# Moving a load's mark, three list products and the first expert's weight splits in a fused convolution and mixture-of-experts kernel

## The chip, the core and the metric

The kernel runs on one core of one Trainium2 chip. Its time is the device time of one execution in microseconds; of the kernel before there are three runs, 1089.16 to 1090.57 us, median 1089.47 us. One more execution was taken with the profiler: 1089.97 us, of which 1088.1 us lie between its first and last instruction.

The engines: PE multiplies matrices, ACT and DVE work on vectors, POOL issues indirect transfers and does small copies, SP only issues transfers. Each engine runs its own queue in order.

## The reference

```python
# x: 8 x 2880 x 192; weight: 8 heads x 7 taps; 4 groups x 4 experts; w1 192 x 1024, w2 1024 x 192
w = softmax(weight, taps)                       # one band of 7 taps for each head of 24 columns
x = causal_conv(x, w).reshape(23040, 192)
g_idx = argmax(x @ w_group); g_w = softmax(x @ w_group)[g_idx]
e_idx = argmax(x @ w_expert[g_idx]); e_w = softmax(...)[e_idx]
out[token] = g_w * e_w * (relu(x @ w1[g_idx, e_idx]) @ w2[g_idx, e_idx])
```

Each token goes to one of 16 experts; everything is fp32.

## The kernel before

**Routing.** The 23040 tokens are cut into 192 blocks of 120, and these into 18 units of 4, 8, 12, 8, 8, 8 and then 12 blocks (units 0 to 17). `unit(u)` is a generator: it loads x (`load_unit`), convolves head by head (L516, one matmul group per head, evicted by ACT at L525), transposes (`turn_a` L540, `turn_b` L548), computes router logits (`logits_of`, L581/L584, for units 0 to 5, by quads of four blocks; `logits` L560/L562 and `logits_back` L572 from unit 6), takes argmax and softmax on DVE (L621 to L652, with the copy `ohp` on POOL, L639), stores its convolved rows to DRAM (`xcd`, L654), counts positions (L663/L664 and L667 to L706 on DVE, whose last large product is `ohl`, L695) and then makes its list of token numbers: `list_products` (L716 on PE, L724 and L726 on DVE, a scatter to the table `idtab` by POOL, L729). Up to three units are alive at once; `step()` advances them in turn by one yield.

**Experts.** A slot is 256 tokens of one expert. `open_slot` reads token numbers from the table (`idp`, L1228, SP), loads the expert's weights (`weights`) and gathers its rows (`gather`, L816, two indirect transfers on POOL). `split_one` does one of four pieces of splitting an expert's weights in a high and a low part: an ACT copy and a DVE subtraction each (L782/L783, L787/L788, L795/L796 twice). Then `turn` transposes the gathered rows (L852 on PE, L857/L858), and `hidden` (L918) and `back` do the products.

**Order at the front.** A first loop runs steps until the first five units are listed (`NEED = 5`); it takes 162 steps, k = 0 to 161. Slots 0 and 1 are opened behind it, then 108 more steps follow (`AHEAD - TB`), then the first slot's `turn`, and from there on expert work and routing steps alternate. What is traced in this order is arranged for each engine by a planner that goes by trace order and by its own estimate of when inputs are there; `hold` and `pin` keep an instruction in traced order on its engine, and `tc.issue_after(ins)` puts the instructions of a block behind `ins` on the same engine (no semaphore).

**The places of the change.** `gated_load` (L247/L248) writes a tiny mark on DVE into the x buffer, kept in order, so that the x load behind it can't start sooner; `KX` is the step at which the loads of units 7 and 8 are marked. `LATE` is the number of steps between a unit's positions and the tracing of its list (units 0 to 3; unit 4 lists at once and flushes what waits). `KPRE` gives the steps at which the first two experts' weights are loaded (60, 110) and the first expert's splits are traced (150, 155, 160; the fourth, at 162, is never reached and falls behind the 108 steps). `GPIN` names the slots whose gathers are put behind the latest traced `ohp` copy on POOL.

Of the kernel before, what the change touches and what calls it, by code (L numbers as in the profile page):

```python
# [24 lines left out]
BI = 2  # L25
# [4 lines left out]
LH = 32  # L30
# [7 lines left out]
def conv_moe_kernel(  # L38
# [10 lines left out]
    nc = tc.nc  # L49
# [41 lines left out]
    for b in range(B):  # L91
        k = b * NB
# [33 lines left out]
    QGB = 3  # L126
    AHEAD = 112
    LISTLAG = 8
    LATE = 8
    HOLD = 2  # L130
    LAG_S = 1
    PTURN = (4, 6)
# [20 lines left out]
    FRH = 0  # L153
    UG = [0, 5, 6, 1, 5, 8, 0, 5, 6, 0, 5, 7, 0, 5, 6, 2, 5, 10]
    SK = [8, 8, 6, 11, 10, 9, 9]
    KPRE = [60, 150, 155, 160, 162, 110]
    KX = 142
    SEV = 99
    TB = 4
    HGAP = 3  # L160
# [108 lines left out]
    for q, (p0, r0, n) in enumerate(((0, 0, P), (0, P, D2), (D2, P, D2))):  # L269
        c = min(q, 1)  # L270
# [14 lines left out]
    def clear_table():  # L285
# [9 lines left out]
        out=tri, in_=ones, pattern=[[1, P]], compare_op=ALU.is_gt, fill=0.0, base=0, channel_multiplier=-1,  # L295
# [12 lines left out]
    for nb in sorted({n for _, n in units}):  # L308
# [34 lines left out]
        out=sel, in_=ident.rearrange("p (e l) -> p e l", e=E), axis=AX.X, op=ALU.add)  # L343
    nc.gpsimd.iota(io[:, 0:1], pattern=[[0, 1]], base=0, channel_multiplier=1)
    nc.vector.tensor_scalar(
        out=io[:, 1:2], in0=io[:, 0:1], scalar1=LE - 1, scalar2=None, op0=ALU.bitwise_and)
# [6 lines left out]
    k = 0  # L353
    while k < E:
        n = CAPS.count(CAPS[k])
# [8 lines left out]
    for g in range(NSK):  # L364
        nc.sync.dma_start(
            out=skew[0:R, g * HG:(g + 1) * HG],
# [7 lines left out]
    for v in (3, 4):  # L374
        n = units[v][1]
# [45 lines left out]
    for h in range(H):  # L421
        nc.scalar.activation(
            out=band[0:R, h], in_=skew[0:R, h, BT - 1::-1], func=AF.Exp, bias=wm[0:R, h:h + 1],
# [27 lines left out]
        xg.append((t[:, 0:XE], t[:, XE:XE + XW]))  # L451

    GATED = (7, 8, 9, 10)
    GPIN = (2, 3)
    ohp_last = [None]
    list_last = [None]
    shared = []
    bands = {}

# [4 lines left out]
    def unit(u, pre=None):  # L464
        c0, nb = units[u]
# [40 lines left out]
        for h in range(H):  # L506
            if h:
                yield
            cs = slice(h * HC, (h + 1) * HC)
            ps = bank("c")  # L510
            if split:
                ops = ((bands["h"], xh), (bands["l"], xh), (bands["h"], xl))
            else:
                ops = ((band, xin),)
            for i, (bb, xx) in enumerate(ops):
                nc.tensor.matmul(  # L516
                    out=ps[0:BT, 0:nb * HC], lhsT=bb[0:R, h, :], rhs=xx[0:R, :, cs],
                    start=i == 0, stop=i == len(ops) - 1,
                )
            pv = ps[0:BT, 0:nb * HC].rearrange("p (b c) -> p b c", c=HC)  # L520
            xo = xc[0:BT, 0:nb, 1 + h * HC:1 + (h + 1) * HC]
            if u < CEU and h in CEH:
                nc.vector.tensor_copy(out=xo, in_=pv)
            else:
                nc.scalar.activation(out=xo, in_=pv, func=AF.Copy)  # L525
# [4 lines left out]
        k = min(range(QRING - NQ, -1, -1), key=lambda k: max(quads[k:k + NQ]))  # L530
# [45 lines left out]
        def logits_of(q):  # L576
            lgp = bank("l")
            for i in range(HQ):
                o = lgp[0:BT, 2 * i * REPL * NL:2 * (i + 1) * REPL * NL].rearrange("p (j n) -> p j n", j=2)
                for j in range(2):  # L580
                    nc.tensor.matmul(  # L581
                        out=o[:, j].rearrange("p (r n) -> p r n", n=NL), lhsT=ta[:, q, 2 * i + j],
                        rhs=wr[:, 0, 0:NL].unsqueeze(1).broadcast_to([P, REPL, NL]), start=j == 0, stop=False)
                nc.tensor.matmul(  # L584
                    out=o[:, :, 0:NL], lhsT=tb[:, q, i], rhs=wrb[:, :, 0:NL], start=False, stop=True)
            read.add((u, q))
            nc.scalar.activation(
                out=lg[0:BT, q * QB:(q + 1) * QB],
                in_=lgp[0:BT, 0:QB * REPL * NL].rearrange("p (b n) -> p b n", b=QB)[:, :, 0:NL], func=AF.Copy)
# [15 lines left out]
        Q = BT  # L605

        def bc(a, n):
# [16 lines left out]
            out=sc, in0=dd, scalar=0.0, in1=prio[0:Q].unsqueeze(1).broadcast_to([Q, M, EG]),  # L624
# [9 lines left out]
            out=ohx[0:Q], in0=ohv[:, :, 1:NG, :].rearrange("p b g e -> p g e b"),  # L634
# [59 lines left out]
        ohr = rt.tile([P, UB // BI, LH, BI], F16, name="ohr")[:, 0:NP]  # L694
# [17 lines left out]
        def list_products():  # L712
            pl = bank("l")
            nrep = REPO if u < REPU else 1
            for k in range(nb):
                nc.tensor.matmul(  # L716
                    out=pl[:, 0:nrep * LH].rearrange("p (r n) -> p r n", r=nrep),
                    lhsT=ohl[0:Q, k // BI, :, :, k % BI].rearrange("p e l -> p (e l)"),
                    rhs=ohr[0:Q, k // BI, :, k % BI].unsqueeze(1).broadcast_to([Q, nrep, LH]),
                    start=k == 0, stop=k == nb - 1,  # L720
                )
            lv5 = rt.tile([P, LH], F32, name="lv5", bufs=1)
            lsi = rt.tile([P, LH], I32, name="lsi", bufs=4)
            nc.vector.tensor_scalar(  # L724
                out=lv5, in0=pl[:, 0:LH], scalar1=0.0, scalar2=float(BIG), op0=ALU.is_equal, op1=ALU.mult)
            nc.vector.scalar_tensor_tensor(  # L726
                out=lsi, in0=pl[:, 0:LH], scalar=float(t0 - 1), in1=lv5, op0=ALU.add, op1=ALU.add)

            list_last[0] = nc.gpsimd.indirect_dma_start(  # L729
                out=TABV, out_offset=bass.IndirectOffsetOnAxis(ap=rowi.bitcast(U32), axis=0),  # L730
                in_=lsi, in_offset=None,
            )
            finished(u)

        if u < NEED - 1:
            waiting.append((done[0] + LATE, list_products))
        else:
            while waiting:
                waiting.pop(0)[1]()
            list_products()  # L740
# [62 lines left out]
    def split_one(W, k=None):  # L803

        if W["todo"] and k in (None, 4 - len(W["todo"])):
            W["todo"].pop(0)()
# [4 lines left out]
    def gather(ids, known, n=2, m=P):  # L811
        xs = xg[nslot[0] % NXG]
        nslot[0] += 1
        for t in range(n):
            with tc.issue_after(ohp_last[0].ins) if nslot[0] - 1 in GPIN else nullcontext():
                nc.gpsimd.indirect_dma_start(  # L816
                    out=xs[t][0:m, 0:XW], out_offset=None, in_=xcd[0:known, :],
                    in_offset=bass.IndirectOffsetOnAxis(ap=ids[0:m, t, 0:1].bitcast(U32), axis=0),
                    bounds_check=known - 1, oob_is_err=False,
                )  # L820
        return xs
# [328 lines left out]
    done = [0]  # L1150
# [3 lines left out]
    def step():  # L1154

        if routed[0] < NU and len(live) < lead[1] and (not live or max(live, key=lambda a: a[0])[1] >= (lead[0] or SK[min(routed[0], len(SK)) - 1])):
            u = routed[0]
            live.append([u, 0, unit(u, xin0 if u == 0 else None)])
            routed[0] += 1
        if not live:  # L1160
            return
        done[0] += 1
        while waiting and waiting[0][0] <= done[0]:
            waiting.pop(0)[1]()
        cur = live.pop(0)
        cur[1] += 1
        try:
            next(cur[2])
            live.append(cur)
        except StopIteration:  # L1170
            pass
# [110 lines left out]
    def open_slot(i):  # L1282
        if i >= len(plan) or i in opened:
            return
        pi, v, at, n, m = plan[i]
        if closing:
            wait[0] -= 1
            if wait[0] <= 0 or closing[0] == pi:
                open_portion(closing.pop())
        while pi not in idps:  # L1290
            step()
            if closing:
                open_portion(closing.pop())
        rate[0] = max(
            [(stages_to(portions[q][0]) - done[0]) / (max(starts[q] - MARGIN - i, 1) * 2 * NF)
             for q in starts if q not in idps] + [0.0])
        if at:
            W = opened[i - 1][0]
        elif pi == LASTP:
            W = weights(*tail_regs(lambda c: tab[0][0:1, v, c:c + 1], 2))  # L1300
        else:
            e = portions[pi][1][v][0]
            if pi == 0 and e in pre:
                W = pre.pop(e)
                with tc.issue_after(opener[0].ins):
                    while W["more"]:
                        W["more"].pop(0)()
            elif i <= 3:
                with tc.issue_after(opener[0].ins):
                    W = weights(e * D, e * F)  # L1310
            else:
                W = weights(e * D, e * F)
        lists(pi, v + IDN)
        ids = idps[pi][v][:, at:at + n]
        known = sum(n for _, n in units[:portions[pi][0]]) * BT
        opened[i] = (W, ids)
        gathered[i] = gather(ids, known, n, m)

    pre = {}
    rooms, factors = {}, {}  # L1320
    k = 0
    while routed[1] < portions[0][0]:
# [16 lines left out]
        clear_half(0)  # L1339
    open_slot(0)  # L1340
    open_slot(1)
    for k in range(AHEAD - TB):
        step()
    while opened[0][0]["todo"]:
        split_one(opened[0][0])
    if TB:
# [201 lines left out]
```

## Time and profile before

| | us |
|---|---|
| median of three runs | 1089.47 |
| profiled execution | 1089.97 |
| its span | 1088.1 |
| PE busy | 1043.7 (96%) |
| DVE busy | 677.6 (62%) |
| ACT busy | 618.4 (57%) |
| POOL busy | 531.7 (49%) |

The time that PE does not work lies nearly all at the front, while the first units are routed and the first experts start, and at the very end. Idle time of an engine counts only where the next work of PE waits for it. In the rows below "idle before" in brackets is the time that the engine waited, and the arrow names what ended the wait.

### The profile page before, as it was taken

To read this page: it belongs to the slowest core of one execution; us is meant where nothing else is said; L and a number is where in the kernel's file an instruction comes from. 1 tells how busy PE (TensorE), PEld (TensorE's weight loads), DVE (VectorE), ACT (ScalarE), POOL (GpSimd) and SP (SyncE) were. 2 spreads that over 40 slices of the span, in tenths; PEclk is the share of its full clock that TensorE was granted. 3 is DMA by queue.
4 is the path that set the end of the run, shared out by engine and by line. 5 is a ranking of instruction groups with operands and counts; after the bars stand their busy time and mean duration, and the time that the engine had idled before them with its cause. 6 is when DMAs were issued, how large, how long until landed. Compare 5 with 4: busy or idle time off the path is not lost.

```text
span 1088.1 us, 20687 instructions
## 1 busy us (share of the span) xinstructions
PE 1043.7 (96%) x7116; PEld 980.7 (90%) x7116; DVE 677.6 (62%) x1650; ACT 618.4 (57%) x1380; POOL 531.7 (49%) x677
## 2 busy tenths in 40 slices
PE   6878999999999999999999999999999999999996
PEld 5756888998999899899999999999999999999996
DVE  4667878886777766656464646556466465655652
ACT  5566687886666645545453645545455455555552
POOL 3233343543333446655554553555556656667542
PEclk9989999999999999999999999999999999999998
DMA  8866897886674343432231313133132233233200
GB/s 210 233 174 161 194 271 201 230 224 186 161 167 133 93 116 89 115 85 65 75 83 53 100 41 90 56 95 97 42 96 69 77 92 104 66 87 98 68 26 23
DMA packets 120281, 126.40 MB, mean 116 GB/s; under 512 B 20619, under 2 KB 106896, under 8 KB 120170
## 3 DMA queue, kind: packets, MB, share of 16 engines
q1 hardware_dynamic: 72682, 71.24, 24.7%
q0 software_dynamic: 24160, 35.99, 11.9%
q10 hardware_dynamic: 23328, 17.80, 6.7%
q8 instruction: 57, 0.93, 0.4%
q14 instruction: 54, 0.44, 0.1%
HBM read 89.03 MB, written 36.07 MB: 115 GB/s over the span
## 4 chain that ended last, share of the span: by engine, by line
PE 76%; DMA 7%; DVE 6%; issue 5%; ACT 3%; POOL 3%; POOLq 0%; SPq 0%; ACTq 0%; DVEq 0%
PE ph L888 26%; PE po L902 10%; PE pm L902 7%; PE ph L918 7%; PE po L906 5%; PE po L936 4%; PE pm L906 3%; PE pm L516 3%; PE po L940 2%; DMA out<-ys,idp 2%; DMA xin<-in_x 2%; PE ph L852 1%; POOL out L955 1%; POOL xg L816 1%; PE pm L540 1%
## 5 line engine op out<-in xcount | busy, mean ns | idle before, releaser
L955 POOL DMA_INDIRECT out<-ys,idp x187 | 214.2, 1146 | 258.2 <-DVE ys L965 203.9
L892 DVE SCALAR_TENSOR_TENSOR hl<-ph,hh 128x360 fp32r<-128x360 f32 (+13 forms) x328 | 189.5, 584 | 197.9 <-ACT hh L891 174.8
L891 ACT ACTIVATE hh<-ph 128x360 fp32r<-128x360 f32 (+13 forms) x328 | 166.3, 515 | 207.9 <-PE ph L888 182.4
L816 POOL DMA_INDIRECT xg<-xcd,idp x187 | 226.7, 1212 | 70.6 <-issue 36.6
L902 PE MATMUL po<-cw,hh 128*120 128x384 f32 (+6 forms) x656 | 209.9, 357 | 0.0
L888 PE MATMUL ph<-xa,wf 128*128 128x360 f32 (+13 forms) x656 | 182.3, 359 | 0.0
L888 PE MATMUL ph<-xc,wf 128*128 128x360 f32 (+13 forms) x656 | 176.4, 350 | 1.7 <-DVE xc L864 1.7
L906 PE MATMUL po<-cw,hl 128*120 128x192 f32 (+6 forms) x656 | 164.7, 251 | 0.0
L902 PE MATMUL pm<-cw,hh 128*120 128x384 f32 (+6 forms) x440 | 147.1, 356 | 0.0
L936 PE MATMUL po<-cw,hh 128*128 128x384 f32 x400 | 134.5, 386 | 0.1
L888 PEld LDWEIGHTS ph<-xc,wf 128*128 128x128 f32 x656 | 118.8, 189 | 11.1 <-DVE xc L864 1.9
L906 PEld LDWEIGHTS po<-cw,hl 128*120 128x120 f32 (+6 forms) x656 | 121.7, 186 | 3.0
L918 PE MATMUL ph<-xa,wf 128*128 128x256 f32 x600 | 118.8, 306 | 5.1 <-DVE wf L783 2.2
L902 PEld LDWEIGHTS po<-cw,hh 128*120 128x120 f32 (+6 forms) x656 | 120.4, 184 | 2.8
L888 PE MATMUL ph<-lts,wf 128*128 128x360 f32 (+13 forms) x328 | 115.0, 351 | 0.0
L906 PE MATMUL pm<-cw,hl 128*120 128x192 f32 (+6 forms) x440 | 110.4, 251 | 0.0
L888 PEld LDWEIGHTS ph<-xa,wf 128*128 128x128 f32 x656 | 100.9, 189 | 1.3
L940 PE MATMUL po<-cw,hl 128*128 128x192 f32 x400 | 101.6, 254 | 0.0
L918 PEld LDWEIGHTS ph<-xa,wf 128*128 128x128 f32 x600 | 88.7, 192 | 11.6 <-DVE wf L783 2.4
L924 DVE SCALAR_TENSOR_TENSOR hl<-ph,hh 128x512 fp32r<-128x512 f32 x100 | 68.2, 686 | 44.0 <-ACT hh L923 38.2
L918 PE MATMUL ph<-xb,wf 128*128 128x256 f32 x400 | 81.9, 286 | 2.8 <-DVE xb L864 2.0
L923 ACT ACTIVATE hh<-ph 128x512 fp32r<-128x512 f32 x100 | 59.5, 598 | 43.6 <-PE ph L918 40.1
(277 smaller groups left out, 1905.2 us busy)
## 6 DMA issues: line engine op xcount, KB each, us to landing
rawc<-in_moe_w SPq DMA_DIRECT2D x66, 384.0 KB
raw<-in_moe_w SPq DMA_DIRECT2D x33, 512.0 KB
xcd<-xc ACTq DMA_DIRECT2D x13, 1085.6 KB
raw<-in_moe_w SPq DMA_DIRECT2D x33, 256.0 KB
xin<-in_x SPq DMA_DIRECT2D x7, 1134.0 KB
xin<-in_x SPq DMA_DIRECT2D x5, 1039.5 KB
xg<-xcd,idp POOLq DMA_INDIRECT x187
out<-ys,idp POOLq DMA_INDIRECT x187
```

Source lines behind the costliest of these rows:

```text
L816: nc.gpsimd.indirect_dma_start(out=xs[t][0:m, 0:XW], out_offset=None, in_=xcd[0:known, :], in_offset=bass.IndirectOffsetOnAxis(ap=ids[0:m, ...
L888: nc.tensor.matmul(out=hp, lhsT=W[wgt][:, fs], rhs=xx[:, 0:n], start=i == 0, stop=i == len(ops) - 1)
L891: nc.scalar.activation(out=hh, in_=hp, func=AF.Relu)
L892: nc.vector.scalar_tensor_tensor(out=hl, in0=hp, scalar=0.0, in1=hh.bitcast(F32), op0=ALU.max, op1=ALU.subtract,)
L902: nc.tensor.matmul(out=oo[t][0:m, 0:2 * D], lhsT=hh[:, ts], rhs=cw[:, f].rearrange("p a d -> p (a d)"), start=f == 0, stop=False,)
L906: nc.tensor.matmul(out=oo[t][0:m, 0:D], lhsT=hl[:, ts], rhs=cw[:, f, 0, :], start=False, stop=f == NF - 1,)
L918: nc.tensor.matmul(out=hp[:, j], lhsT=wgt[:, fs], rhs=xx, start=i == 0, stop=i == len(ops) - 1)
L923: nc.scalar.activation(out=hh, in_=hp, func=AF.Relu)
L924: nc.vector.scalar_tensor_tensor(out=hl, in0=hp, scalar=0.0, in1=hh.bitcast(F32), op0=ALU.max, op1=ALU.subtract,)
L936: nc.tensor.matmul(out=oo[t][:, 0:2 * D], lhsT=hh[:, j, ts], rhs=cw[:, f].rearrange("p a d -> p (a d)"), start=f == 0, stop=False,)
L940: nc.tensor.matmul(out=oo[t][:, 0:D], lhsT=hl[:, j, ts], rhs=cw[:, f, 0, :], start=False, stop=f == NF - 1,)
L955: nc.gpsimd.indirect_dma_start(out=outviews[nscat[0] % len(outviews) if view is None else view], out_offset=bass.IndirectOffsetOnAxis(ap=i ...
```

## The change

- `KX` from 142 to 130. The mark for x of units 7 and 8 is traced behind unit 3's positions and unit 4's first logits, where it was behind unit 4's argmax.
- `LATE` from 8 for all to (8, 8, 14, 10). Unit 2's list is traced at step 127 instead of 121, unit 3's at 137 instead of 135.
- `BEHIND`: on PE the list products of unit 1 go behind the latest traced logits, those of units 2 and 3 behind the latest logits and the latest convolution. Counted through the generators these are: unit 1 behind unit 3's first logits; unit 2 behind unit 3's second logits and unit 5's second head; unit 3 behind unit 4's second logits and unit 5's sixth head.
- The four splits of the first expert are not traced at steps 150 to 160, but at steps 2, 8, 14 and 20 of the 108 that follow the opening.
- The gathers of slots 0 and 1 are traced only once a new `ohp` copy is (unit 5's, at step 13 of the 108) and go behind it on POOL.

```diff
-    LATE = 8
+    LATE = (8, 8, 14, 10)
+    BEHIND = ((), ("l",), ("l", "c"), ("l", "c"))
-    KPRE = [60, 150, 155, 160, 162, 110]
-    KX = 142
+    KPRE = [60, 999, 999, 999, 999, 110]
+    FIRST = (2, 8, 14, 20)
+    KX = 130
-    GPIN = (2, 3)
+    GPIN = (0, 1, 2, 3)
+    recent = {}
...
-                nc.tensor.matmul(
+                recent["c"] = nc.tensor.matmul(
                     out=ps[0:BT, 0:nb * HC], lhsT=bb[0:R, h, :], rhs=xx[0:R, :, cs],
...
-                nc.tensor.matmul(
+                recent["l"] = nc.tensor.matmul(
                     out=o[:, :, 0:NL], lhsT=tb[:, q, i], rhs=wrb[:, :, 0:NL], start=False, stop=True)
...
         def list_products():
             pl = bank("l")
             nrep = REPO if u < REPU else 1
-            for k in range(nb):
+            with ExitStack() as queued:
+                for kind in BEHIND[u] if u < len(BEHIND) else ():
+                    queued.enter_context(tc.issue_after(recent[kind].ins))
+                for k in range(nb):
...
-            waiting.append((done[0] + LATE, list_products))
+            waiting.append((done[0] + LATE[u], list_products))
...
-        gathered[i] = gather(ids, known, n, m)
+
+        def fetch():
+            gathered[i] = gather(ids, known, n, m)
+
+        if i < 2:
+            fetches.append(fetch)
+        else:
+            fetch()
...
     open_slot(0)
     open_slot(1)
+    newest = ohp_last[0]
     for k in range(AHEAD - TB):
         step()
+        while fetches and ohp_last[0] is not newest:
+            fetches.pop(0)()
+        if k in FIRST:
+            split_one(opened[0][0])
     while opened[0][0]["todo"]:
         split_one(opened[0][0])
```

## Rows read from the trace of the kernel before

**Rows 1.** Windows: busy us of each engine (instructions), granted clock, DMA share, GB/s.

```profile
63.40:74.30 10.90, 6.44 (x28) 5.41 (x28) 4.74 (x17) 4.40 (x11) 1.25 (x3) 0.69 0.83 268
74.30:93.20 18.90, 16.55 (x120) 10.86 (x119) 13.65 (x56) 14.28 (x36) 9.47 (x10) 1.00 0.61 148
59.40:98.20 38.80, 29.35 (x188) 20.98 (x186) 27.09 (x102) 25.18 (x62) 12.12 (x15) 0.91 0.64 173
98.20:200.00 101.80, 95.86 (x734) 87.59 (x735) 81.95 (x192) 75.80 (x147) 39.14 (x38) 0.99 0.88 229
600.00:800.00 200.00, 200.00 (x1290) 195.35 (x1289) 113.90 (x240) 106.86 (x246) 107.42 (x147) 1.00 0.29 76
```

**Rows 2.** Waits of PE, 36 to 100 us: total us, times, longest us.

```profile
PE ph L516 <- DMA xin<-in_x: 4.5, 1, 4.5
PE pm L716 <- DVE ohl L695: 2.8, 2, 1.5
PE ph L918 <- DVE xa L858: 1.7, 1, 1.7
PE ph L716 <- DVE ohl L695: 1.7, 1, 1.7
```

**Rows 3.** Timeline of PE, 55 to 74 us: start, us, line, what.

```profile
55.59 0.84 PE L716 MATMUL pm<-ohr,ohl 120*128 120x192 f16 x8 [1.25 <-DVE ohl L695]
56.28 0.58 PE L581 MATMUL pm<-wr,ta 128*120 128x100 f32 x4
...
61.41 0.66 PE L581 MATMUL po<-wr,ta 128*120 128x100 f32 x4
...
62.69 0.72 PE L516 MATMUL ph<-wf,band 126*120 126x288 f32 x2
67.88 1.28 PE L516 MATMUL ph<-xin,band 126*120 126x288 f32 x2 [4.46 <-DMA xin<-in_x]
68.96 1.49 PE L716 MATMUL pm<-ohr,ohl 120*128 120x192 f16 x8
...
71.24 0.97 PE L581 MATMUL pm<-wr,ta 128*120 128x100 f32 x4
...
73.51 0.93 PE L516 MATMUL pm<-xin,band 126*120 126x288 f32 x2
```

**Rows 4.** Timeline of DVE, 54 to 67 us: units 3 and 4, mark, splits.

```profile
54.84 0.69 DVE L695 TENSOR_TENSOR ohl<-ohp,oh 120x1024 f16<-120x1024 f16 x1
...
57.95 0.32 DVE L621 TENSOR_REDUCE mx<-lg 120x40 f32<-120x160 f32 x1 [1.06 <-ACT lg L587]
...
60.80 0.07 DVE L248 MEMSET xin<- 1x2 f32 x2
...
61.35 1.22 DVE L783 TENSOR_TENSOR wf<-raw,wf 128x1024 fp32r<-128x1024 f32 x1
...
62.97 1.21 DVE L788 TENSOR_TENSOR wf<-raw,wf 64x1024 fp32r<-64x1024 f32 x1
...
66.11 0.69 DVE L695 TENSOR_TENSOR ohl<-ohp,oh 120x1024 f16<-120x1024 f16 x1
```

**Rows 5.** Timeline of SP at the mark: the load of unit 7's x.

```profile
60.92 0.34 SPq L236 DMA_DIRECT2D xin<-in_x  x1
```

**Rows 6.** Timeline of all engines: a split's copy, POOL beside DVE, the last split.

```profile
59.99 1.07 ACT L782 ACTIVATE wf<-raw 128x1024 fp32r<-128x1024 f32 x1
...
74.21 2.80 POOL L401 TENSOR_SCALAR wf<-ident 64x1024 fp32r<-64x1024 f32 x1 [1.56 <-DMA idtab<-lsi,rowi]
74.37 1.07 DVE L622 TENSOR_TENSOR dd<-lg,mx 120x160 f32<-120x160 f32 x1
...
95.09 0.95 DVE L796 TENSOR_TENSOR cw<-rawc,cw 128x768 fp32r<-128x768 f32 x1
```

**Rows 7.** Timeline: the last gather of slots 0 and 1, the first transpose of slot 0.

```profile
82.23 1.01 POOL L816 DMA_INDIRECT xg<-xcd,idp  x1 [0.30 <-issue]
...
93.16 0.27 PE L852 MATMUL pm<-ident,xg 128*128 128x128 f32 x1
```

More of the change, by code (lines that the diff above doesn't have):

```diff
@@ L714, in list_products @@
             nrep = REPO if u < REPU else 1
-            for k in range(nb):
[L716 to L721, printed above, removed]
+            with ExitStack() as queued:
+                for kind in BEHIND[u] if u < len(BEHIND) else ():
+                    queued.enter_context(tc.issue_after(recent[kind].ins))
+                for k in range(nb):
+                    nc.tensor.matmul(
+                        out=pl[:, 0:nrep * LH].rearrange("p (r n) -> p r n", r=nrep),
+                        lhsT=ohl[0:Q, k // BI, :, :, k % BI].rearrange("p e l -> p (e l)"),
+                        rhs=ohr[0:Q, k // BI, :, k % BI].unsqueeze(1).broadcast_to([Q, nrep, LH]),
+                        start=k == 0, stop=k == nb - 1,
+                    )
             lv5 = rt.tile([P, LH], F32, name="lv5", bufs=1)
@@ L1316, in open_slot @@
         opened[i] = (W, ids)
-        gathered[i] = gather(ids, known, n, m)
+        def fetch():
[4 more added lines that the diff above has]
+            fetch()
     pre = {}
+    fetches = []
     rooms, factors = {}, {}
```

## The prediction

> **What bounds the kernel now.** I read the page's busy shares first, then the windows, PE's waits, and the timelines of PE, DVE, SP and POOL where those waits lie. PE is the bound: from 600 to 800 us it is busy 200.00 of 200.00 us at full clock [rows 1], so work that it does earlier at the front comes off the end, if nothing takes it back in between. At the front it is not full: from 63.4 to 74.3 us it is busy 6.44 of 10.90 us at a mean granted clock of 0.69, from 74.3 to 93.2 us 16.55 of 18.90 [rows 1]. The waits name the causes [rows 2]: 4.5 us for the x load of unit 7, three waits for `ohl` before list products (2.8 us in two, 1.7 us in one), 1.7 us for the subtraction `xa` of the first slot.
>
> The timeline shows how the longest arises. The convolution of unit 7 stands on PE ahead of unit 4's list and starts at 67.88, after 4.46 us of waiting [rows 3]; its load was issued at 60.92 [rows 5], right behind the mark at 60.80 [rows 4]. From mark to convolution that is 7.08 us, and the mark is what set it. Behind the wait PE runs at the lower level, 1.2 GHz instead of 2.4: the 8-block list takes 1.49 us at 68.96 and 0.84 at 55.59, and the logits with their second half go from 71.24 to 73.51 (2.27 us), where the same go from 61.41 to 62.69 (1.28 us) [rows 3].
>
> **The change part by part.**
>
> *The mark.* It stands behind what is traced before it: now behind unit 4's argmax, at 60.80. Moved to step 130 it comes behind unit 3's positions, whose last large product ends at 54.84 + 0.69 = 55.53 [rows 4]; I put it at 55.6, and x is usable at 55.6 + 7.1 = 62.7. PE has run out of other work at 67.88 - 4.46 = 63.42 [rows 3], 1.2 us sooner with the next part, so 62.2. About 0.5 us of the wait is left: gain 4.46 - 0.5 = 3.9 us. It is worth this only if PE isn't stopped there by something else, namely unit 4's list, whose `ohl` ends at 66.11 + 0.69 = 66.80 [rows 4]: see the splits. The moved load issues the same transfers on SP; the queue holds nothing between them and the opening, and DMA is used 0.83 in the stretch that they leave [rows 1].
>
> *The clock.* If PE doesn't stand still for 4.46 us, I expect no fall. From 67.88 to 73.51 it does one convolution, the list, another convolution and two halves of logits in 5.63 us [rows 3]. At full clock: two convolutions at half of 1.08, the list 0.69 (from 55.59 to 56.28), the logits 1.28 [rows 3], together 3.05. Gain 2.6 us; nothing if a like wait stays.
>
> *The list products.* Unit 3's now stands ahead of unit 4's second logits: PE waits 1.25 us for `ohl`, does the list at 55.59, and only then the logits at 56.28 [rows 3], so that DVE stands idle for them until 57.95 [rows 4]. Behind the logits the list has their 1.28 us as cover: gain 1.2 us on PE, and unit 4's argmax can start when unit 3's `ohl` is done, at about 56.0, so 1.9 us sooner. For units 1 and 2 the edges ask for what the order of before has already: what they name was issued ahead of these lists. Their waits, 1.5 and 1.7 us [rows 2], I leave as they are: gain 0, at best 3.2 if the later place of unit 2's list reorders more, at worst -1.7 if it does so the other way (the longest such wait once more).
>
> *The splits, where they go from.* Two subtractions, 1.22 and 1.21 us, stand at 61.35 and 62.97 inside unit 4's chain to `ohl` [rows 4]. Without them and with the argmax 1.9 us sooner, `ohl` ends at 66.80 - 2.43 - 1.9 = 62.5, as early as PE gets to the list. So the x wait is not replaced by a wait for `ohl`; the two belong together, and if the splits stayed, some 2.4 us of the 3.9 would be lost again. The opening, behind unit 4's list, comes some 6 us sooner.
>
> *The splits, where they go to.* The fourth one's subtraction, 0.95 us at 95.09 [rows 6], stands now ahead of the first slot's `xa`, for which PE waits 1.7 us [rows 2]: gain 0.95, and up to 2.6 if the rest of that wait and its slow clock go too. The others come new into the stretch between opening and first slot: on DVE 1.22 + 1.21 + 0.95 = 3.4 us. DVE is busy 13.65 of 18.90 us there, ACT 14.28 of 18.90 [rows 1]. Bounds: 0, if they fall into the idle 5.25 us; 3.4, if all lie on the path. I take 2.4, since the two that stand in unit 4's chain today were both on the path in whole and the two traced at steps 2 and 8 come ahead of unit 5's argmax in the same way. The ACT copies (1.07 us for the largest [rows 6]) I count at nothing: the copies precede the subtractions and the evictions that they hold up have several PSUM buffers; if ACT bound the stretch they would cost about as much as the subtractions, which the upper end covers.
>
> One row of this stretch speaks against the place: `clear_half` on POOL runs 2.80 us from 74.21, and the DVE subtraction that starts beside it at 74.37 takes 1.07 us [rows 6], where an instruction over the same 120x160 values takes 0.32 [rows 4]; it is 0.75 longer, but it ends at 75.44, long before POOL does at 77.01. The splits' subtractions will stand near this instruction. The Trainium skill says in "SBUF — State Buffer", section "SBUF: two separate sides", that a DVE operation with two SBUF inputs and a GpSimd operation that reads SBUF share one pair of ports as an exclusive lock for the whole instruction. By that rule DVE should have been shut out for all of POOL's 2.80 us, so the trace agrees that there is a price, not with its size.
>
> *The gathers.* Today the last gather of slots 0 and 1 is issued at 82.23 and slot 0's rows are first used at 93.16 [rows 7], a cover of 10 us. Behind unit 5's copy they shift with the opening and with unit 5, both sooner. Cost 0; without that cover each gather costs about the 1.01 us of its issue on POOL [rows 7] and its landing.
>
> *Sum.* 3.9 + 2.6 + 1.2 + 0.95 - 2.4 = 6.25 us. The profiled execution of 1089.97 us becomes 1083.7; it lies 0.5 us above the median of the runs, so I forecast 1083.2. DVE allows this: from 59.4 to 98.2 us it is busy 27.09 of 38.80 us [rows 1], so up to 11.7 us could go before it is full. Behind 98.2 us the relations stay: splits, loads and gathers of later slots hang on the first slot's progress, and DMA, 0.88 busy up to 200 us [rows 1], gets two x loads and the first weight buffers sooner. That is the least certain step.
>
> **The rivals.**
>
> *Both waits for unit 1 and 2 lists go too.* The new edges leave PE other work there: 1083.2 - 3.2 = 1080.0. Against it: the named work was done already.
>
> *The lock in whole.* A subtraction of the splits waits out `clear_half`, 2.80 us instead of the 0.75 of the row [rows 6], and unit 5 behind it: 2.05 us more, 1085.3. It is the rule named above as a mechanism of this kernel; the row bears it out only in part.
>
> *The wait travels with the mark.* PE's order is planned with an estimate of the load that is too short: today unit 7's convolution is reached 63.42 - 60.80 = 2.6 us after the mark. If the plan keeps that distance, the 4.46 us and the slow clock stay: 0 + 0 + 1.2 + 0.95 - 2.4 = -0.25, so 1090.2, or 1089.7 against the median. Against it: the hole that drew the convolution there is the wait for unit 4's `ohl`, and ahead of it PE has other work without a gap.
>
> *Slower.* The plan sets that convolution right behind the mark, at about 56 us on PE, ahead of unit 3's list and unit 4's logits: then PE waits the whole 7.08 us there, 2.6 more than today, unit 4's chain waits with it, and the splits cost their 2.4: 1089.97 + 2.6 - 1.2 - 0.95 + 2.4 = 1092.8, or 1092.3 against the median. It decides from where less than 2.6 us of PE work lie between mark and convolution.
>
> **How the numbers follow.** Forecast 0.56, lists 0.08, lock 0.10, travelling wait 0.14, slower 0.12. The measurement can tell about 0.2% of this kernel, 2.2 us, from no change. Faster by more: 0.56 + 0.08 + 0.10 = 0.74; within: 0.14; slower: 0.12. The range: from 1083.2 the free splits give 2.4 less and the rest of the `xa` wait 1.6 less, 1079.2, and with some of the list waits 1078; upwards the splits in whole and the lock give 1086.3, and the travelling wait is taken in with a little room, 1090.5. What is left out is the slower case and the far end of the list case.
>
> **What would show it.** Right: the x load issued near 56 us, PE's wait for x under 1 us, a granted clock of 1.00 through 60 to 80 us, unit 4's logits ahead of unit 3's list, the opening's read of the table some 6 us sooner, slot 0's first transpose near 87 us instead of 93.16, and the same distance of about 6 us still there at 200 and at 600 us. Wrong: a wait for x of 4 us or more anywhere, a clock under 0.9 in that stretch, DVE full from opening to first slot with PE waiting for it, or a gain at the first slot that is gone by 200 us, which would mean that DMA or DVE behind it set the pace.

## The result, and the profile after

The changed kernel takes 1081.7 us in the median of four runs (1080.2 to 1082.43), where the kernel before took 1090.02 us beside it (1089.16 to 1092.17): a ratio of 0.991, 95% interval 0.9886 to 0.9933. The forecast was 1083.2 us, so direction and range hold, and the gain is 8.3 us where 6.25 were summed. The profiled execution is 1081.58 us long, 1079.7 of it between first and last instruction. Three single runs of the kernels below took 1661 to 2081 us; no ratio counts them.

Windows of the changed kernel, over stretches of [rows 1] and over 140 to 200 us; columns as there, with the granted clock and the DMA share ahead of GB/s.

```profile
63.40:74.30 10.90, 7.89 (x54) 6.12 (x54) 8.35 (x24) 9.25 (x21) 5.10 (x4) 1.00 0.44 103
74.30:93.20 18.90, 15.24 (x105) 9.74 (x105) 12.86 (x50) 13.35 (x33) 6.13 (x8) 0.91 0.65 163
600.00:800.00 200.00, 200.00 (x1287) 195.37 (x1286) 113.30 (x238) 105.18 (x242) 105.14 (x144) 1.00 0.29 81
140.00:200.00 60.00, 60.00 (x482) 54.77 (x482) 48.30 (x111) 47.65 (x96) 25.10 (x23) 1.00 0.92 240
```

From 63.4 to 74.3 us the granted clock is 1.00 instead of 0.69, and PE gets through 54 instructions where it did 28. From 74.3 to 93.2 us the stretch became worse: 15.24 us busy instead of 16.55, clock 0.91 instead of 1.00. PE is still the bound later (200.00 of 200.00 us).

Waits of PE in the changed kernel, 36 to 100 us: total us, times, longest us.

```profile
PE pm L722 <- ACT lg L576: 1.9, 1, 1.9
PE pm L722 <- DVE ohl L698: 1.8, 2, 1.2
PE ph L563 <- ACT ta L544: 1.8, 1, 1.8
PE ph L666 <- DVE cum L644: 1.7, 1, 1.7
PE ph L722 <- DVE ohl L698: 1.3, 1, 1.3
```

Against [rows 2]: the wait for x is gone from the list, the waits for `ohl` are shorter (1.8 and 1.3 us instead of 2.8 and 1.7), the waits for `ta` and `cum` (1.8 and 1.7 us) are new, and that for `lg` has grown from 0.6 to 1.9 us. All of PE's waits in this stretch, the smaller ones with them, come to 9.9 us, where they were 14.0. (The changed file's lines stand 2 to 6 further down: L516 is L519, L716 is L722, L918 is L924.)

Where the lead arises shows when the same event of both traces is set side by side (start in us):

| event | before | after | lead |
|---|---|---|---|
| unit 3's first argmax | 44.13 | 44.35 | -0.2 |
| unit 4's first argmax | 57.95 | 54.20 | 3.8 |
| unit 7's first convolution | 67.88 | 60.47 | 7.4 |
| unit 4's list on PE | 68.96 | 63.47 | 5.5 |
| table read by the opening | 74.15 | 69.62 | 4.5 |
| slot 0's first transpose | 93.16 | 89.81 | 3.4 |
| slot 0's first expert product | 95.54 | 91.17 | 4.4 |
| 1st scaling of an output tile (ACT) | 117.15 | 111.14 | 6.0 |
| 3rd | 134.14 | 130.46 | 3.7 |
| 11th | 193.20 | 186.09 | 7.1 |
| 34th | 351.12 | 344.09 | 7.0 |
| 180th | 1047.86 | 1039.09 | 8.8 |

So there are three phases: 5.5 us won up to unit 4's list, 2.1 of them lost by the first slot, and over 5 us won after that, with a loss of 2.3 us between the first and the third scaling.

PE and DVE of the changed kernel up to unit 4's list (start, us, line, what).

```profile
48.61 0.07 DVE L250 MEMSET xin<- 1x2 f32 x2
...
48.87 0.57 PE L584 MATMUL pm<-wr,ta 128*120 128x100 f32 x4
...
50.78 1.18 PE L722 MATMUL ph<-ohr,ohl 120*128 120x192 f16 x12 [1.35 <-DVE ohl L698]
...
53.09 0.64 PE L584 MATMUL pm<-wr,ta 128*120 128x100 f32 x4
...
54.20 0.32 DVE L624 TENSOR_REDUCE mx<-lg 120x40 f32<-120x160 f32 x1
...
55.10 0.69 DVE L698 TENSOR_TENSOR ohl<-ohp,oh 120x1024 f16<-120x1024 f16 x1
...
55.85 0.84 PE L722 MATMUL pm<-ohr,ohl 120*128 120x192 f16 x8 [0.59 <-DVE ohl L698]
...
59.84 0.19 PE L666 MATMUL ph<-cum,tri 120*128 120x16 bf16 x1
...
60.11 0.17 DVE L670 TENSOR_TENSOR off<-ph,eoff 128x16 f32<-128x16 f32 x1 [1.50 <-PE ph L667]
...
60.47 0.70 PE L519 MATMUL ph<-xin,band 126*120 126x288 f32 x2
...
62.72 0.69 DVE L698 TENSOR_TENSOR ohl<-ohp,oh 120x1024 f16<-120x1024 f16 x1
...
63.47 0.84 PE L722 MATMUL pm<-ohr,ohl 120*128 120x192 f16 x8
```

The mark stands at 48.61 us, ahead of unit 2's `ohl` (49.77). Unit 4's second quad of logits, which stood behind unit 3's list (56.28 [rows 3]), now begins ahead of unit 2's list (48.87) and goes on ahead of unit 3's (53.09). Unit 4's argmax starts at 54.20, ahead of unit 3's `ohl` (55.10). Unit 7's convolution finds x there at 60.47, and unit 4's list runs at full clock (0.84 us, before 1.49 [rows 3]).

All engines of the changed kernel, from opening to the first slot.

```profile
66.24 1.22 DVE L789 TENSOR_TENSOR wf<-raw,wf 128x1024 fp32r<-128x1024 f32 x1 [1.48 <-ACT wf L788]
...
67.13 1.19 POOL L735 DMA_INDIRECT idtab<-lsi,rowi  x1 [5.24 <-DMA idtab<-lsi,rowi]
...
69.69 2.80 POOL L403 TENSOR_SCALAR wf<-ident 64x1024 fp32r<-64x1024 f32 x1 [1.37 <-DMA idtab<-lsi,rowi]
69.80 1.11 DVE L632 TENSOR_TENSOR oh<-sc,mx 120x160 f32<-120x160 f32 x1
...
71.34 0.87 ACT L801 ACTIVATE cw<-rawc 128x768 fp32r<-128x768 f32 x1
71.45 1.06 DVE L653 TENSOR_SCALAR sg<-ss 120x8 f32<-120x8 f32 x1
71.86 0.93 DVE L802 TENSOR_TENSOR cw<-rawc,cw 128x768 fp32r<-128x768 f32 x1
...
73.38 0.32 ACTq L657 DMA_DIRECT2D xcd<-xc  x1
...
81.61 0.42 ACT L528 ACTIVATE xc<-ph 120x288 f32<-120x288 f32 x1 [2.42 <-DMA xcd<-xc]
82.32 0.40 DVE L624 TENSOR_REDUCE mx<-lg 120x60 f32<-120x240 f32 x1 [5.27 <-ACT lg L576]
```

Windows of the changed kernel, 4 us each, over the same place.

```profile
68.00:72.00 4.00, 2.49 (x14) 1.50 (x13) 3.93 (x11) 3.98 (x9) 2.63 (x2) 1.00 0.34 23
72.00:76.00 4.00, 1.63 (x16) 0.94 (x19) 3.90 (x19) 3.20 (x10) 2.99 (x4) 0.90 0.93 265
76.00:80.00 4.00, 4.00 (x31) 2.29 (x24) 0.91 (x3) 3.08 (x5) 2.83 (x4) 0.68 1.09 268
80.00:84.00 4.00, 2.09 (x20) 1.75 (x18) 1.58 (x5) 1.95 (x6) 0.00 (x0) 1.00 0.46 128
```

This is where the lead shrinks. While the splits run, ACT is busy 3.98 and DVE 3.93 of 4.00 us, and PE only 2.49, then 1.63, and the clock behind it is 0.68. Unit 5's convolved rows are stored at 73.38, in ACT's queue behind the splits' copies, and behind weight loads that SP issued from 70.12 us on. A later eviction waits for that store until 81.61, and from 80 to 84 us no engine is busy for much over half of the time.

### The profile page after: what moved, and what is told of

The parts are those of the page before. It is cut to its first block, busy times and chain, and to the rows that moved or that the text cites. A ratio compares the mean times of both kernels' runs of the same rounds, so it can differ in the third digit from the quotient of the medians.

```text
span 1079.7 us, 20690 instructions
## 1 busy us (share of the span) xinstructions
PE 1041.8 (96%) x7116; PEld 979.3 (91%) x7116; DVE 675.8 (63%) x1650; ACT 618.2 (57%) x1380; POOL 534.0 (49%) x677
## 4 chain that ended last, share of the span: by engine, by line
PE 85%; DVE 6%; DMA 4%; ACT 2%; issue 1%; POOL 0%; SPq 0%; POOLq 0%; DVEq 0%; ACTq 0%
PE ph L894 28%; PE po L908 10%; PE ph L924 9%; PE pm L908 8%; PE po L942 6%; PE po L912 5%; PE pm L912 4%; PE pm L519 4%; PE po L946 3%; DMA out<-ys,idp 2%; PE ph L858 1%; PE pm L543 1%; PE pm L722 1%; DMA xcd<-xc 1%; DMA xin<-in_x 1%
## 5 line engine op out<-in xcount | busy, mean ns | idle before, releaser
L961 POOL DMA_INDIRECT out<-ys,idp x187 | 216.5, 1158 | 264.2 <-DVE ys L971 210.3
L924 PE MATMUL ph<-xa,wf 128*128 128x256 f32 x600 | 118.4, 305 | 2.4 <-DVE wf L789 2.4
L924 PEld LDWEIGHTS ph<-xa,wf 128*128 128x128 f32 x600 | 88.2, 191 | 8.6 <-DVE wf L789 2.8
L924 PE MATMUL ph<-xb,wf 128*128 128x256 f32 x400 | 81.5, 285 | 3.3 <-DVE xb L870 2.0
```

The costliest lines, as they stand in the source:

```text
L924: nc.tensor.matmul(out=hp[:, j], lhsT=wgt[:, fs], rhs=xx, start=i == 0, stop=i == len(ops) - 1)
L961: nc.gpsimd.indirect_dma_start(out=outviews[nscat[0] % len(outviews) if view is None else view], out_offset=bass.IndirectOffsetOnAxis(ap=i ...
```

## The experiments

All ratios are to the kernel before on the same chip, with 95% intervals; the gain is (1 - ratio) x 1090 us. The line of the whole change is that of its second measurement, beside the experiments. The three sets of experiments ran on three chips, so kernels of different sets are compared by their ratios alone. A kernel with parts alone is the changed file with the other parts set back.

| kernel | ratio | interval | gain, us | PE's wait for x |
|---|---|---|---|---|
| whole change | 0.991 | 0.9895 to 0.9926 | 9.8 | none |
| without the mark | 0.9977 | 0.9961 to 0.9992 | 2.5 | 4.0 |
| without the lists | 0.9957 | 0.9944 to 0.997 | 4.7 | none |
| without the splits | 0.9925 | 0.9907 to 0.9943 | 8.2 | none |
| without the gathers | 0.9936 | 0.9917 to 0.9955 | 7.0 | none |
| mark alone | 0.995 | 0.9936 to 0.9965 | 5.5 | none |
| lists alone | 0.9963 | 0.9945 to 0.9981 | 4.0 | 3.7 |
| splits alone | 0.9962 | 0.9941 to 0.9984 | 4.1 | 0.2 |
| mark and lists | 0.9931 | 0.9905 to 0.9958 | 7.5 | none |
| whole, mark at step 138 | 0.9973 | 0.995 to 0.9996 | 2.9 | 3.8 |
| whole, splits at 36 to 54 | 0.9904 | 0.9889 to 0.9919 | 10.5 | none |
| that, mark at step 138 | 0.9947 | 0.9922 to 0.9971 | 5.8 | 2.9 |

The start of an execution varies by some us from one to the next (unit 3's first argmax lies between 42.09 and 48.32 us in the profiled ones), so where times of different traces are compared below, they are counted from that event.

First theory, the prediction's: the mark is the largest part, the lists a small one, and the splits cost something at their new place. Rival: the lists or the splits carry the gain. Four kernels put one part of the changed kernel back.

**Without the mark.**

```diff
-    KX = 130
+    KX = 142
```

> The changed kernel with only the mark put back (step 142). First theory, the wait for x is the largest part of the gain: the mark stands behind unit 4's argmax again, near 58 us, x lands near 65, PE waits 2 to 4 us for it with unit 4's list behind, and runs some 4 us at the lower clock; 1085 to 1087 us, against 1081.7 with the whole change. Rival, PE would stand still there anyway for unit 4's ohl (ready at 63.4 in the changed kernel): the wait only changes its name, 1082 to 1083 us.

Measured: 0.9977. The mark is worth some 7 us here (9.8 - 2.5), somewhat above the first theory's 3.3 to 5.3 and far from the rival's 0.3 to 1.3. Timeline of DVE and PE of this kernel:

```profile
61.10 0.07 DVE L250 MEMSET xin<- 1x2 f32 x2
...
69.58 0.75 PE L519 MATMUL ph<-xin,band 126*120 126x288 f32 x2 [3.98 <-DMA xin<-in_x]
70.14 1.48 PE L722 MATMUL pm<-ohr,ohl 120*128 120x192 f16 x8
```

The old picture is back: a wait of 3.98 us, and the list behind it at the lower level (1.48 us).

**Without the lists.**

```diff
-    LATE = (8, 8, 14, 10)
-    BEHIND = ((), ("l",), ("l", "c"), ("l", "c"))
+    LATE = (8, 8, 8, 8)
+    BEHIND = ((), (), (), ())
```

> The changed kernel with LATE 8 for all and no BEHIND. First theory, unit 4's logits ahead of unit 3's list are worth 1.2 us of PE and bring unit 4's argmax 1.9 us sooner or more: without them 1083 to 1085 us. Rival, the time that unit 4 gains is lost again behind the opening, where unit 5's stored rows hold the evictions of unit 8: 1081.5 to 1082 us.

Measured: 0.9957. The lists are worth about 5 us, where the prediction had 1.2. From unit 3's to unit 4's first argmax this kernel takes 14.02 us, the whole change 9.85, the kernel before 13.82. This distance goes with the lists: it is 9.75 to 10.71 in all kernels of the study that have them and 13.80 to 14.06 in all that don't. No run separates the later steps (`LATE`) from the edges (`BEHIND`).

**Without the splits.**

```diff
-    KPRE = [60, 999, 999, 999, 999, 110]
-    FIRST = (2, 8, 14, 20)
+    KPRE = [60, 150, 155, 160, 162, 110]
+    FIRST = ()
```

> The changed kernel with the first expert's splits back ahead of the opening. First theory, both places cost about the same on the path (2.4 us in unit 4's chain, 2.4 us in unit 5's) and only the fourth split's 0.95 us and its slow clock at the first slot differ: 1082.5 to 1084.5 us. Rival one, the new place is the dearer (ACT is full from 68 to 72 us in the changed kernel and PE waits 1.8 us for it): 1079.5 to 1081 us. Rival two, the mark is worth nothing without the splits moved: 1087 us or more.

Measured: 0.9925, 1.6 us above the whole change, with intervals that overlap. PE waits 1.51 us for unit 4's `ohl` and 1.6 us for `xa` in this kernel, and not in the whole change, but the fuller stretch behind the opening is absent too. So what the splits' new place is worth in the whole change is not settled by this run. It does settle something about the store of unit 5's rows. ACT of this kernel:

```profile
71.08 0.32 ACTq L657 DMA_DIRECT2D xcd<-xc  x1
...
80.45 0.42 ACT L528 ACTIVATE xc<-ph 120x288 f32<-120x288 f32 x1 [1.39 <-DMA xcd<-xc]
```

No copy of a split stands between opening and store here, but three weight loads (69.38 to 70.65 us on SP) do. The store comes 27.03 us behind unit 3's argmax (whole change 29.03), and an eviction still waits 1.39 us for it.

**Without the gathers.**

```diff
-    GPIN = (0, 1, 2, 3)
+    GPIN = (2, 3)
...
-        if i < 2:
+        if i < 0:
             fetches.append(fetch)
```

> The changed kernel with the gathers of slots 0 and 1 issued at the opening and not put behind the copy. They then stand ahead of unit 5's copy on POOL and hold it by about 5 us; DVE idles 5 us at that place in the changed kernel. First theory, this cover hides it: 1081.2 to 1082.2 us, no change. Rival, unit 5's list and everything in DVE's order behind it come later: 1083 to 1085 us.

Measured: 0.9936, 2.8 us above the whole change, at the edge of what the intervals separate. POOL and DVE of this kernel:

```profile
79.06 1.01 POOL L822 DMA_INDIRECT xg<-xcd,idp  x1 [0.31 <-issue]
80.12 0.30 POOL L642 CAST ohp<-ohx 120x128 f16<-120x128 bf16 x1
...
80.45 0.69 DVE L698 TENSOR_TENSOR ohl<-ohp,oh 120x1024 f16<-120x1024 f16 x1 [3.27 <-POOL ohp L642]
```

With the four gathers in front, unit 5's copy is done only at 80.12, and DVE waits 3.27 us for it. In the whole change the copy is at 72.55 and `ohl` at 76.36. The edge has a use that the prediction didn't give it: it lets the copy past the gathers.

The second set took the whole change once more as a reference, each of two parts alone, and the splits later.

> The changed kernel once more, unaltered, for a comparison on the same chip with the three below. All theories: 0.988 to 0.993 of the kernel before, 8 to 13 us less.

Measured: 0.991 (1078.42 to 1082.48 us). Its trace has the same waits (9.4 us of PE's in 36 to 100 us).

**The mark alone** (kernel before, with `KX` at 130).

```diff
-    KX = 142
+    KX = 130
```

> The kernel before with the mark alone moved to step 130. First theory, the mark is worth most of the gain by itself: PE does unit 7's convolutions where it waited, the clock stays, unit 4's list goes ahead as soon as its ohl is there (66.8 in the kernel before, so 2 us sooner): 4 to 6 us less than before. Rival, mark and splits need each other (the wait for ohl takes the place of the wait for x): 1 to 2.5 us less.

Measured: 0.995. The prediction had said that mark and splits belong together and that some 2.4 us would be lost with the splits in unit 4's chain. PE does wait for `ohl` there, 1.05 us, and unit 4's list runs at the lower level (1.46 us), but 5.5 us remain.

**The lists alone** (kernel before, with `LATE` and `BEHIND`).

```diff
-    LATE = 8
+    LATE = (8, 8, 14, 10)
+    BEHIND = ((), ("l",), ("l", "c"), ("l", "c"))
```

> The kernel before with the lists' new places alone. First theory: unit 4's argmax comes 3 us sooner, but the wait for x behind the late mark stays and takes it back: 0 to 1.5 us less than before. Rival, the mark itself stands behind unit 4's argmax and moves with it, so that the gain goes through: 2.5 to 4 us less.

Measured: 0.9963. The mark, still traced behind unit 4's argmax, follows it to 56.62 us; the wait for x is 3.7 us.

**The splits later**, at steps where unit 5's rows are already stored.

```diff
-    FIRST = (2, 8, 14, 20)
+    FIRST = (36, 42, 48, 54)
```

> The changed kernel with the first expert's four splits at steps 36, 42, 48 and 54 behind the opening instead of 2, 8, 14 and 20. In the changed kernel DVE idles 5.3 us from 77 to 82 us, ACT is full from 68 to 72, and unit 5's store takes 8.2 us from 73.4 because four weight loads, set free by the splits, go ahead of it. First theory, the splits and the loads that they set free crowd unit 5: 2 to 4 us less than the changed kernel. Rival, the store is slow for the gathers and the loads need the early splits: no change, or up to 2 us more where the second expert's weights come too late.

Measured: 0.9904, 1078.61 us (1077.85 to 1081.74). Windows of this kernel over the place of the loss:

```profile
68.00:72.00 4.00, 1.31 (x12) 0.70 (x14) 3.69 (x20) 2.58 (x8) 3.20 (x3) 0.92 0.59 94
72.00:76.00 4.00, 4.00 (x26) 1.75 (x18) 2.61 (x4) 3.95 (x6) 3.08 (x4) 0.65 0.63 166
76.00:80.00 4.00, 3.85 (x30) 3.09 (x29) 3.79 (x10) 4.00 (x12) 1.36 (x3) 1.00 0.98 316
80.00:84.00 4.00, 3.92 (x25) 1.58 (x24) 3.83 (x20) 1.98 (x7) 1.53 (x3) 1.00 0.56 164
```

Unit 5's rows are stored at 69.16 us, no eviction waits for that, and PE is busy 3.92 of 4.00 us at 80 to 84 instead of 2.09. The store comes 27.07 us behind unit 3's argmax, as in the kernel without the splits' move, but here the weight loads follow it:

```profile
74.06 0.48 SPq L767 DMA_DIRECT2D raw<-in_moe_w  x1
```

So of the eviction's wait, the weight loads ahead of the store are the likely part, beside the copies that make it later. PE's wait for `ta` and the fall of the clock do not go away: PE is busy 1.31 of 4.00 us at 68 to 72 (a wait of 2.6 us for `ta`), and the clock behind it is 0.65. Counted from unit 3's first argmax, the 34th scaling comes at 296.23 us, against 299.74 and 298.80 in the two traces of the whole change; at the 60th 0.6 and 1.3 us of that are left.

What the place costs can be read from unit 4's list on PE to slot 0's first transpose: 22.39 to 24.58 us in the five traces with the splits ahead of the opening, 25.64 to 28.78 in the seven with splits at steps 2 to 20, and 24.15 and 25.34 in the two with later ones. So the loss behind the opening came in good part from the place of the splits. In the timed runs the intervals of this kernel and of the whole change overlap widely; a better kernel is not shown.

The last set asked how far the mark's place decides, and whether parts add. It ran on a chip where the kernel before itself varied from 1083.2 to 1095.62 us, and its intervals are wider.

**The mark at step 138**, close to where the prediction had put it.

```diff
-    KX = 130
+    KX = 138
```

> The whole change with the mark at step 138 instead of 130; on DVE it then stands behind unit 3's list numbers, near 57.4 us, where the changed kernel has it at 48.61 (and where the prediction had put it at 55.6). First theory: all that counts is whether x is there when PE is free for it; a load takes some 7 to 8 us, so x is usable at 64.5 to 65.5, PE is free at about 61 to 63, and it waits 2 to 4 us with a slow clock behind: 2 to 4 us above the whole change, 1083.5 to 1085.5. Rival: the early mark has a price of its own, since the x loads at 55 to 63 us slow down the table scatters and the opening; then the later mark gives an opening sooner by 1 to 2 us and no loss: 1080 to 1081.5.

Measured: 0.9973. Timeline of DVE and PE of this kernel:

```profile
61.43 0.07 DVE L250 MEMSET xin<- 1x2 f32 x2
...
70.08 1.28 PE L519 MATMUL ph<-xin,band 126*120 126x288 f32 x2 [3.78 <-DMA xin<-in_x]
```

This execution started later: its unit 3's argmax is at 48.32, so the mark stands 13.1 us behind it (whole change 4.3, before 16.7; the prediction's 55.6 would be 11.5). PE waits 3.78 us for x, and most of the gain is gone. The rival had a true part: with the mark early, the table's scatters run against the x loads. DMA issues of the whole change, then of this kernel, 44 to 76 us: count and median us from issue to landing. In each, the median is that of one scatter, unit 2's; the trace doesn't tell when the others landed.

```profile
idtab<-lsi,rowi POOLq DMA_INDIRECT x4, 6.6
```

```profile
idtab<-lsi,rowi POOLq DMA_INDIRECT x4, 2.2
```

But the price is outweighed: from unit 3's argmax the table is read after 25.27 us in the whole change and after 27.84 here.

**Late splits, mark at step 138.**

> As the kernel with splits at steps 36 to 54 (1078.6), with the mark at step 138 instead of 130. First theory: again 2 to 4 us above the same kernel with the early mark, 1080.5 to 1082.5. Rival: the scatters are freed and the opening comes sooner, 1077 to 1078.5.

Measured: 0.9947, with a wait of 2.9 us for x: the same answer at the other place of the splits. The sizes, 4.7 us here and 6.9 us above, are larger than the 2 to 4 expected, though the intervals are too wide to exclude 4.

**Mark and lists**, with splits and gathers as before.

> The mark and the lists of the change; splits and gathers where they stood before. The two alone gave 5.5 and 4.0 us. Theory that the parts add: 9.5 us, 1080.5, so that the new places of splits and gathers are worth nothing by themselves. Rival, from the two runs that put one of them back (1083.7 and 1084.1): they are worth 2 to 4 us together, since the splits' subtractions again stand in unit 4's chain to ohl (2.4 us) and POOL does gathers ahead of unit 5's copy: 1083.5 to 1086. Unit 4's ohl should end near 65 us and PE wait about 2 us for it if the rival holds.

Measured: 0.9931, a gain of 7.5 us; the interval, 4.6 to 10.4 us, takes in both the sum of the two alone (9.5 us) and 4 us less than that. Of what the rival named, PE's wait for unit 4's `ohl` is there, 1.51 us, and it ends at 63.30 us on PE.

**The splits alone.** The expectation names the gathers too; in the kernel they stood where they were before, only the splits had moved.

```diff
-    KPRE = [60, 150, 155, 160, 162, 110]
+    KPRE = [60, 999, 999, 999, 999, 110]
+    FIRST = (2, 8, 14, 20)
```

> The kernel before with the new places of splits and gathers alone; mark and lists as before. The prediction's steps: 0.95 gained at the fourth split, 2.4 lost at the new place, the x wait and the slow clock as before: 1.4 us slower, 1091. Parts that add (whole change less mark and lists alone, 9.8 - 5.5 - 4.0 = 0.3): 1089 to 1090. Rival, that unit 4's chain is freed of 2.4 us and this comes through by itself: 1086.5 to 1088.

Measured: 0.9962, 4.1 us faster, where the prediction's own steps give 1.4 slower. PE of this kernel:

```profile
66.11 1.46 PE L722 MATMUL pm<-ohr,ohl 120*128 120x192 f16 x8 [1.52 <-DVE ohl L698]
...
70.46 0.72 PE L519 MATMUL ph<-xin,band 126*120 126x288 f32 x2 [0.19 <-DMA xin<-in_x]
```

With unit 4's chain free of splits, PE's order puts the list ahead of unit 7's convolution, and the wait for x falls to 0.19 us although the mark is as late as before (62.07, which is 16.6 us behind unit 3's argmax; before 16.7). PE still waits 1.52 us for `ohl`, and the list runs at the lower level (1.46 us).

**What the table says.** The parts don't add. Lists and splits alone gave 4.0 and 4.1 us, but together, with the gathers and without the mark, 2.5: a gap of 5.6 us, where the intervals together leave some 3.5. Mark, lists and splits alone sum to 13.6 us, the whole gave 9.8; this difference alone would be at the edge of the intervals. The likely reason, which no run isolates, is that the planner makes a new order for each combination, and that whether PE meets a convolution whose x isn't there depends on that order.

## Why the prediction came out as it did

**The mark.** Right in kind: the wait for x is gone, and the part is the largest by both measures (7.3 us taken out, 5.5 alone), though its intervals overlap those of the lists. Two terms under it were wrong and offset each other. I put the mark at 55.6 us, behind all that is traced earlier; it stands at 48.61. Unit 2's `ohl`, traced some 17 steps before the mark, stands behind it in DVE's queue, so tracing the mark later did not put it behind all that is traced earlier, as I had taken for given. And I let PE be free at 62.2; it reaches the convolution at 60.47. With my own place of the mark, the load of 7.1 us [rows 3 to 5] would have left 62.7 - 60.5 = 2.2 us of waiting and not 0.5. The run with the mark at step 138, 1.6 us behind my place, shows 3.8. So the forecast is owed partly to luck: a mark 7 us earlier than derived.

**The clock.** Right: 1.00 from 63.4 to 74.3 us. The work summed at 3.05 us (a convolution, the list, another convolution and the logits) takes 3.17 us, from 62.67 to 65.84. But the low clock came back elsewhere (0.68 at 76 to 80 us, about 0.5 from 116 to 122 behind a wait of 1.97 us), which was in no term.

**The lists.** The term of the sum that was mis-sized most: 1.2 us, against about 5 (whole less the run without) or 4.0 (alone). Two steps failed. "Unit 4's argmax can start when unit 3's `ohl` is done" set 1.9 us; in the trace the argmax, at 54.20, runs ahead of that `ohl`, at 55.10. And by "gain 0, since what the edges name was issued ahead already" I read only the edges, and gave the later place of unit 2's list no effect beyond a bound of 3.2 us. PE of the kernel before:

```profile
52.48 1.85 PE L516 MATMUL ph<-wf,band 126*120 126x192 f32 x8
```

These eight convolution matmuls ran ahead of unit 4's second logits. In the changed kernel six of them (1.53 us at 53.72) run behind, and four of the logits' own matmuls, some 0.4 us, come ahead of unit 2's list. With unit 3's list and its wait (0.69 + 1.25 us) that is an estimate of 3.9 us, and unit 4's argmax came 3.8 us sooner instead of 1.9. Which of the new steps and edges brings which part was not tried. The rival case of the list waits (1080.0) was close in time, but not by its mechanism: those waits only fell from 2.8 and 1.7 to 1.8 and 1.3 us.

**The splits, where they go from.** The step "without them `ohl` ends at 62.5" missed: it ends at 63.41. The 2.43 us of subtractions did leave the chain, but what is late next was not named: the matmul of unit 4's counts, which stands at 59.84 in PE's queue though its input is done at 57.82, and DVE waits 1.50 us for it. PE did not wait for it, since it reached the list only at 63.47. The claim that mark and splits need each other fell: the mark alone gave 5.5 us.

**The splits, where they go to.** Counting DVE's 2.4 us and nothing for ACT was near in size and wrong in its reason. ACT is as full as DVE, the first subtraction waits 1.48 us for its copy, and the store of unit 5's rows slid 2 us behind the copies and behind weight loads. PE's wait for `ta`, 1.8 us here, is not the splits' alone: it is 2.6 us with the later splits, and 1.4 and 1.3 in two kernels with the splits ahead of the opening. By the lead, 5.5 us at unit 4's list and 3.4 at the first transpose, the stretch cost 2.1 us, near the 2.4; my expected 87 us for the first transpose was 89.81. Alone the splits' move gains 4.1 us; in the whole change it is 1.6, with overlapping intervals.

**The opening.** "Some 6 us sooner" became 4.5: unit 4's scatter went out at 67.13, 2.4 us behind its list numbers (before 0.8 us), because an earlier scatter to the table, issued beside the x loads, landed only then. I had counted the moved load as free for SP's queue and looked no further along the DMA.

**The fourth split and `xa`.** Right: between the first transpose and the first product the lead grows from 3.35 to 4.37 us, 1.0 against 0.95. It goes on to 6.0 us at the first scaling; together that is about the "up to 2.6" of the bound.

**Behind the first slot.** "The relations stay" was too cautious. From 140 to 200 us PE is busy 60.00 of 60.00 us; in the kernel before:

```profile
140.00:200.00 60.00, 57.39 (x452) 52.43 (x451) 47.09 (x108) 47.86 (x96) 23.05 (x23) 1.00 0.89 244
```

That is 2.6 us of PE's waits in later routing units. Ahead of that, 2.3 us were lost between the first and the third scaling, where the clock of the changed kernel falls at 116 us and that of the kernel before does not (last section). The last 1.7 us, between the 38th and the 52nd scaling, are this trace's alone: the second trace of the whole change, counted from unit 3's argmax, leads the kernel before by 8.3 us at the 11th scaling and by 8.3 at the last. Why the later units fit better was not tried.

**The lock.** `clear_half` stands beside unit 5's small instructions now: two of them take 1.11 and 1.06 us, where the first takes 0.32 and the second 0.17 elsewhere. Only the first held DVE: its successor starts 1.04 us behind it instead of 0.24 to 0.27, while the second's starts 0.08 us behind it as elsewhere. So the price is some 0.8 us, near the 0.75 of the row. The splits' own subtraction at 71.86 shows none (0.93 us). The Trainium skill ("SBUF — State Buffer", section "SBUF: two separate sides") has the port locked for the whole instruction; the trace disagrees, since DVE instructions with two inputs, the one at 69.80 among them, begin and end within POOL's 2.80 us.

So the total was right with right signs for mark and clock, an underestimate of the lists and of the later gain, and a loss behind the opening that was of the expected size for other reasons. That these errors left the sum within 2.1 us of the measured gain is in part luck.

## What to carry to other kernels

When an edit moves an instruction in an order that a planner makes, a sum over the places of before is only a start: ask for each engine what overtakes it, because here the lists' new places let another unit's logits pass a list and six convolution matmuls, and brought its argmax forward by twice what the sum had. For a gated load, work out when the consumer will be reached after the other edits, not before them, and put the mark a whole load time ahead of that. When filling a gap, count the second engine too, the DMAs in its queue and the loads that go ahead of them: here a store behind ACT's copies and weight loads held up an eviction by 2.42 us, and DVE was idle for 5.27 (2.71 at the same place before).

## What the runs showed that was not expected

- Unit 2's small scatter to the table took 6.6 us from issue to landing beside the x loads (DMA share 0.96 to 1.03 from 52 to 64 us), against 2.2 us in the three traces with later loads that tell its landing.
- Like waits don't bring like clocks. At the third slot's first products PE waits for the same subtraction in both kernels, 1.97 us up to 117.11 after and 2.16 us up to 123.44 before. Windows of 2 us at and behind the wait, of the changed kernel and then of the kernel before:

```profile
116.00:118.00 2.00, 0.89 (x4) 0.78 (x5) 2.00 (x4) 1.12 (x2) 2.00 (x2) 0.53 0.19 49
118.00:120.00 2.00, 2.00 (x14) 1.78 (x13) 0.86 (x1) 0.00 (x0) 1.84 (x2) 0.50 0.76 165
```

```profile
122.00:124.00 2.00, 0.56 (x5) 0.52 (x6) 2.00 (x6) 1.32 (x2) 1.70 (x2) 1.00 0.31 99
124.00:126.00 2.00, 2.00 (x21) 1.91 (x19) 1.55 (x4) 0.00 (x0) 1.39 (x2) 1.00 0.51 113
```

  After, PE goes at the lower level (1.2 GHz) until about 123 us; before, it stays at 2.4 GHz. In the second trace of the same changed kernel the fall behind the same wait is about half as long, and with the splits alone a wait of 1.96 us leaves the clock at 1.00. So it is not the length of the wait alone; what makes the difference was not tried.
- Unit 3's first argmax comes at 42.09 to 48.32 us in the 14 traces, and unit 0's already at 16.99 to 21.62. That spread is nearly as large as what the change is worth, so single traces must be aligned at an inner event before their times are compared. Even that event is not rigid: it follows unit 2's argmax by 7.1 to 7.3 us in twelve traces and by 8.7 and 8.9 in two.
